# A fused attention and expert kernel: the second stage's input product in seven block products instead of eight

## The chip, the core and the metric

The kernel runs on one core of a Trainium2 chip. The time is the device time of one execution, from the program's start to its end, in microseconds (us). Five engines take part: TensorE (PE, matrix products), VectorE (DVE), ScalarE (ACT), GpSimd (POOL) and SyncE (SP, which here issues DMAs). Each runs its own instructions in order and waits for others through semaphores.

## The reference

Three parts follow each other. Local attention over 4 batches, 8 heads and 768 positions (a window of 96 positions and 8 global ones, with a linear bias) gives x of 3072 tokens by 512. A gated expert then computes `x2 = ((x @ w1) * (x @ w2)) @ w3 @ w_out`, again 3072 by 512. The second expert is where the change lies:

```
def _moe2_ref(x, w_in, w_out):     # w_in 512 x 2048, w_out 2048 x 512
    h = x @ w_in
    g = h * np.cos(h)
    return (g @ w_out).astype(np.float32)
```

All is float32. The kernel keeps that precision by splitting each operand into a high part in the type fp32r and the remainder, and by computing hi·hi + hi·lo + lo·hi: three matmuls for each product (`mm3`, L387 to L394).

## The kernel before, in words

**Stage one** (attention and the first expert) is one loop of 96 slots over 8 blocks of 384 tokens, written out by hand: each slot holds one unit of attention and 24 matmuls of 384 columns, eight slots of a block for `up` (the products with w1 and w2) and four for `down` (with the folded w3 and w_out). The order of every engine is the order in which the code emits; nothing reorders it. Between them `decode` (a generator, L787 to L822) takes a few steps in every slot: it turns the packed weights into float32, for the second stage too, and stores these as `late_w` in DRAM. `up_copy`, `up_mult`, `up_hi` and `up_lo` (L672 to L688) move the results of `up` out of PSUM; `down_out` (L704) splits x2 into its two parts and stores it to DRAM as `x2s`. In the last block, where no attention is left, `late_load` and `late_split` bring back w_in and most of w_out and split them.

**Stage two** (L981 to L1080) takes 6 blocks of 512 tokens. In each, 16 steps: `hidden(J, m)` computes 128 of the 2048 hidden values (12 matmuls of 512 columns: 4 parts of the inner dimension by 3), `gate` computes h·cos(h) from PSUM with three ACT and five DVE operations, and `project`, two steps later, adds the block's contribution to four output banks in PSUM (12 matmuls). `finish` copies the four banks out at the end of each block. All weights stay in SBUF.

PSUM has eight banks of 128 by 512: in stage two four are hidden (`h_ps`) and four output banks (`o_ps`).

## Time and profile before

| | |
|---|---|
| Median of 3 runs | 1170.9 us (1169.41 to 1172.2) |
| Profiled execution, first to last instruction (span) | 1167.0 us |
| Lies around the span (median less span) | 3.9 us |
| PE busy | 1138.3 us (98%) |
| DVE, ACT, POOL busy | 753.8 us (65%), 593.9 us (51%), 112.3 us (10%) |
| Moved by DMA | 131.12 MB |
| Stage two, first to last matmul | 635.48 to 1158.9 us |

The profile has no device time of its own for the profiled execution, only its span; the 3.9 us are the difference to the median. A busy share tells how long an engine had an instruction in it. For PE these overlap (each matmul is recorded with 389 ns, while the next starts after some 226 ns), so the distance between starts tells its rate. The granted clock (PEclk) is the share of full speed that TensorE was allowed: 1.00 is 2.4 GHz and 0.50 is 1.2 GHz.

### The profile page before, as it was taken

The numbers are of one execution on the slowest core, as the hardware profiler recorded it, in microseconds if no ns is written. First come the engines' busy times: TensorE is split into PE (matmuls) and PEld (weight loads), VectorE is DVE, ScalarE is ACT, GpSimd is POOL, SyncE is SP. The second block draws the span as 40 slices with busy tenths as digits, with TensorE's granted clock in tenths as the row PEclk, the third lists the DMA queues.
The fourth block names the chain that finished last, engine by engine and source line by source line (L and its number), as shares of the span: only waits on it lengthen the run. The fifth ranks groups of instructions, "written<-read, shape, count | busy, mean of one in ns | idle before, by whom it ended". The sixth has DMA issues, their size and how long they took to land.

```text
span 1167.0 us, 17288 instructions
## 1 busy us (share of the span) xinstructions
PE 1138.3 (98%) x6178; PEld 985.5 (84%) x6178; DVE 753.8 (65%) x1696; ACT 593.9 (51%) x1309; POOL 112.3 (10%) x197
## 2 busy tenths in 40 slices
PE   5999999999999999999999999999999999999997
PEld 2455899999999999999999888888888888888885
DVE  7797786767676555555344766666666666666664
ACT  6997786666666555555444533333333333333332
POOL 0000001121112111111132300000000000000000
PEclk9899899999999999999999999999999999999999
DMA  8875686575654424343156302002003003000001
GB/s 267 249 227 179 213 298 215 168 222 158 206 169 152 134 88 141 90 151 95 57 173 210 117 1 89 20 1 89 20 1 96 14 1 102 7 1 36 1 1 39
DMA packets 64783, 131.12 MB, mean 112 GB/s; under 512 B 6576, under 2 KB 27312, under 8 KB 64688
## 3 DMA queue, kind: packets, MB, share of 16 engines
q1 hardware_dynamic: 57648, 117.03, 31.2%
q0 software_dynamic: 6528, 12.58, 3.7%
q8 instruction: 51, 0.84, 0.3%
q14 instruction: 44, 0.36, 0.1%
q10 hardware_dynamic: 512, 0.32, 0.1%
HBM read 102.64 MB, written 27.26 MB: 111 GB/s over the span
## 4 chain that ended last, share of the span: by engine, by line
PE 91%; ACT 3%; DMA 2%; DVE 2%; issue 1%; ACTq 0%; SPq 0%; DVEq 0%
PE mm L392 11%; PE mm L394 11%; PE mm L393 11%; PE o_ps L394 7%; PE h_ps L393 7%; PE o_ps L393 7%; PE h_ps L392 7%; PE o_ps L392 7%; PE h_ps L394 7%; PE x_ps L635 3%; PE mm L854 3%; PE pt_ps L608 2%; PE s_ps L553 1%; PE pt_ps L610 1%; PE s_ps L549 1%; DMA raw<-in_winp 1%
## 5 line engine op out<-in xcount | busy, mean ns | idle before, releaser
L1012 ACT ACTIVATE r<-r 128x512 f32<-128x512 f32 x96 | 60.7, 632 | 149.0 <-DVE r L1008 149.0
L1021 ACT CAST g<-r 128x512 fp32r<-128x512 f32 x96 | 59.6, 621 | 139.5 <-DVE r L1017 139.5
L601 POOL TENSOR_SCALAR e<-e,st 128x232 f32<-128x232 f32 x148 | 72.0, 498 | 499.5 <-DVE st L593 479.3
L517 ACT CAST hh<-qk 128x720 fp32r<-128x720 f32 x74 | 58.7, 794 | 118.4 <-PE s_ps L553 113.3
L1014 DVE SCALAR_TENSOR_TENSOR r<-r 128x512 f32<-128x512 f32 x96 | 66.4, 692 | 70.0 <-ACT r L1012 69.9
L1022 DVE TENSOR_TENSOR g<-r,g 128x512 fp32r<-128x512 f32 x96 | 66.5, 692 | 66.0 <-ACT g L1021 66.0
L392 PE MATMUL mm<-xT,wA 128*128 128x384 f32 x256 | 90.6, 354 | 2.3 <-DVE W L863 2.3
L569 DVE CUSTOM_DVE_ANT_0 e<-s_ps,bias 128x232 f32<-128x232 f32 (+1 forms) x192 | 65.5, 378 | 42.3 <-PE s_ps L553 38.9
L580 ACT ACTIVATE e<-e,top 128x232 f32<-128x232 f32 (+1 forms) x192 | 89.3, 468 | 2.3 <-DVE top L569 2.2
L392 PE MATMUL mm<-ab,W 128*128 128x384 f32 x256 | 89.8, 351 | 0.0
L392 PE MATMUL mm<-xT,wB 128*128 128x384 f32 x256 | 89.5, 350 | 0.0
L394 PE MATMUL mm<-xT,wA 128*128 128x384 f32 x256 | 86.9, 340 | 0.0
L393 PE MATMUL mm<-xT,wA 128*128 128x384 f32 x256 | 86.7, 338 | 0.0
L394 PE MATMUL mm<-xT,wB 128*128 128x384 f32 x256 | 86.2, 337 | 0.0
L394 PE MATMUL mm<-ab,W 128*128 128x384 f32 x256 | 86.2, 337 | 0.0
L393 PE MATMUL mm<-ab,W 128*128 128x384 f32 x256 | 85.9, 336 | 0.0
L393 PE MATMUL mm<-xT,wB 128*128 128x384 f32 x256 | 85.8, 335 | 0.0
L1005 DVE SCALAR_TENSOR_TENSOR r<-kt,h_ps 128x512 f32<-128x512 int32 x96 | 65.7, 684 | 28.5 <-ACT kt L1003 28.1
L1003 ACT ACTIVATE kt<-h_ps 128x512 int32<-128x512 f32 x96 | 57.2, 596 | 34.8 <-PE h_ps L394 34.8
L678 DVE TENSOR_TENSOR ab_f<-mm,a_sb 128x384 f32<-128x384 f32 x64 | 35.5, 555 | 55.8 <-PE mm L394 55.8
L1008 DVE SCALAR_TENSOR_TENSOR r<-kt,r 128x512 f32<-128x512 int32 x96 | 66.4, 692 | 3.3
L854 PE MATMUL mm<-wo,w 128*128 128x512 f32 x128 | 63.8, 632 | 4.5 <-DVE wo L348 4.5
(191 smaller groups left out, 3004.3 us busy)
## 6 DMA issues: line engine op xcount, KB each, us to landing
qk<-in_a_qk SPq DMA_DIRECT2D x74, 360.0 KB, 3.1
v<-in_a_v SPq DMA_DIRECT2D x96, 128.0 KB, 2.9
x2s<-x2t SPq DMA_DIRECT2D x32, 384.0 KB, 3.0
raw<-in_w3p SPq DMA_DIRECT2D x16, 512.0 KB, 5.2
raw<-in_winp SPq DMA_DIRECT2D x16, 512.0 KB, 4.3
late_w<-x SPq DMA_DIRECT2D x32, 256.0 KB, 2.1
raw<-in_wo2p SPq DMA_DIRECT2D x16, 512.0 KB, 3.9
raw<-late_w SPq DMA_DIRECT2D x16, 512.0 KB, 4.2
```

The lines of the kernel that those rows point to most:

```text
L392: nc.tensor.matmul(ps, lhsT=l_hi, rhs=r_hi, start=first and i == 0, stop=False)
L393: nc.tensor.matmul(ps, lhsT=l_hi, rhs=r_lo, start=False, stop=False)
L394: nc.tensor.matmul(ps, lhsT=l_lo, rhs=r_hi, start=False, stop=last and i == n - 1)
L569: nc.vector.tensor_tensor_reduce(out=es[n][:, e, :w], in0=sp[:, e, :w], in1=bias[:, 2 * p + e, :], scale=-0.125, scalar=3.0e38, op0=ALU.ad ...
L580: nc.scalar.activation(es[n][:, e, :w], es[n][:, e, :w], ACTF.Exp, bias=top[:, n, e:e + 1], scale=-1.0, accum_out=sts[n][:, 0, e:e + 1],)
L601: nc.gpsimd.tensor_scalar(x, x, st[:, 1, e:e + 1], 1.0, ALU.mult, ALU.mult)
L854: nc.tensor.matmul(W_ps[m], lhsT=wt["w3", c][:, m * 128:(m + 1) * 128], rhs=wt["wo1", k], start=k == 0, stop=k == M1 - 1,)
L1005: nc.vector.scalar_tensor_tensor(out=r, in0=kt, scalar=-C1, in1=ps, op0=ALU.mult, op1=ALU.add)
L1008: nc.vector.scalar_tensor_tensor(out=r, in0=kt, scalar=-C2, in1=r, op0=ALU.mult, op1=ALU.add)
L1012: nc.scalar.activation(r, r, ACTF.Sin, scale=0.5)
L1014: nc.vector.scalar_tensor_tensor(out=r, in0=r, scalar=-2.0, in1=r, op0=ALU.mult, op1=ALU.mult)
L1022: nc.vector.tensor_tensor(out=t[:, 1, :], in0=r, in1=t[:, 0, :].bitcast(F32), op=ALU.subtract)
```

## The change

The product of x2 (512 by 3072) with w_in is written as a 2x2 block product in the Strassen-Winograd form. One **step** takes a pair of hidden blocks (2 x 128), two halves of the inner dimension (2 x 256) and two blocks of 512 tokens (e = 0 and 1). Eight block products would be needed; seven are computed, each of 6 matmuls (`prod`), into four banks a, b, c, d, and the sums are formed by five additions on DVE and two copies on ACT. A round (q) covers 1024 tokens in 8 steps; there are 3 rounds. In a step, `hj` receives the hidden values of the first token block and `gr` those of the second.

- **Weights.** `combos` makes the seven combinations of each pair's four quarters in stage one, splits them and stores them to `a_s` in DRAM. `piece_load` streams them back, 28 pieces of 512 KB in each round. The last weights (`o2`) are split once, stored to `o2s`, and streamed too, 1 MB for each projection task from the ninth on.
- **x2** is stored unsplit. `x2_steps` forms the four differences of the token blocks and splits seven operands, for round 0 in stage one's last block, for rounds 1 and 2 during the round before.
- **Gate.** h now lies in SBUF, and each gate operation covers 128x1024 instead of 128x512. cos comes from Sin, then Square on ACT, with the factor -2 moved to `finish`.
- **Order.** A projection *task* is 24 matmuls, for one token block and one pair. In a step, the gate of the step before is computed and the task of two steps before is projected between the products; the last step of a round (`dense`) has its task behind its products. Then a loop over `b` projects what is left of the round: two tasks of token block 0, then block 1.
- **Stage one's pace.** `decode` takes 3 steps a slot instead of 1.5 from slot 8 on; the buffer `s` of the decoder has one place less; `up_mult` writes in place, into the tile that `up_copy` of the next slot fills again.

```
+PRODS = [
+    ("a", "B11"), ("b", "T2"), ("c", "T1"), ("d", "T3"), ("a", "B21"), ("c", "B22"), ("d", "T4"),
+]
...
-    x2s = dram.tile([MO, 128, 2, NT], F32R, name="x2s")
-    late_w = dram.tile([2, M2, 128, 512], F32, name="late_w")
+    x2s = dram.tile([MO, 128, NT], F32, name="x2s")
+    late_w = dram.tile([M2, 128, 512], F32, name="late_w")
+    a_s = dram.tile([NP * 7 // 2, 128, 2, 2, 2, 128], F32, name="a_s")
+    o2s = dram.tile([M2, 128, 2, 512], F32, name="o2s")
...
+    def combos(i):
+
+        x1, x2 = (xs.pop(("in", 2 * i + e)) for e in range(2))
+
+        def quarter(x, h):
+            return x[:, h * 256:(h + 1) * 256]
+
+        a11, a12, a21, a22 = (quarter(x, h) for x in (x1, x2) for h in range(2))
+        t = attn.tile([128, 256], F32, tag="comb", name="comb", bufs=1)
+        makes = [
+            (0, a11, None), (4, a12, None), (6, a22, None),
+            (3, t, (a11, a21, ALU.subtract)), (2, t, (a21, a22, ALU.add)),
+            (1, t, (t, a11, ALU.subtract)), (5, t, (a12, t, ALU.subtract)),
+        ]
+        for at, x, make in makes:
+            if make:
+                nc.vector.tensor_tensor(out=t, in0=make[0], in1=make[1], op=make[2])
+                yield
+            o = attn.tile([128, 2, 2, 128], F32R, tag="ap", name="ap", bufs=2)
+            v = x.rearrange("p (k c) -> p k c", k=2)
+            nc.scalar.copy(out=o[:, :, 0, :], in_=v)
+            yield
+            nc.vector.tensor_tensor(
+                out=o[:, :, 1, :], in0=v, in1=o[:, :, 0, :].bitcast(F32), op=ALU.subtract
+            )
+            piece, half = divmod(7 * i + at, 2)
+            nc.sync.dma_start(out=a_s[piece, :, half], in_=o.bitcast(F32))
+            yield
+
...
-        ab_f[m] = moe.tile([128, TB], F32, tag="ab_f", name="ab_f", bufs=1)
-        nc.vector.tensor_tensor(out=ab_f[m], in0=mm_ps.pop("b"), in1=a_sb.pop(m), op=ALU.mult)
+        t = ab_f[m] = a_sb.pop(m)
+        nc.vector.tensor_tensor(out=t, in0=mm_ps.pop("b"), in1=t, op=ALU.mult)
...
-        t = x2t[j, m] = moe.tile([128, 2, TB], F32R, tag="x2t", name="x2t", bufs=1)
-        nc.scalar.copy(out=t[:, 0, :], in_=ps)
-        nc.vector.tensor_tensor(
-            out=t[:, 1, :], in0=ps, in1=t[:, 0, :].bitcast(F32), op=ALU.subtract
-        )
+        t = x2t[j, m] = moe.tile([128, TB], F32, tag="x2t", name="x2t", bufs=1)
+        nc.scalar.copy(out=t, in_=ps)
...
-            rings[key] = {"raw": [(misc, 3)], "x": [(attn, 3)], "s": [(attn, 2)]}
+            rings[key] = {"raw": [(misc, 3)], "x": [(attn, 3)], "s": [(attn, 1)]}
...
+                    if k[1] and k[1][0] == "in" and k[1][1] % 2:
+                        yield from combos(k[1][1] // 2)
...
+        def x2_steps(r0, r1):
+
...
+            less(r1, raw("B22"), r0)
+            yield
+            less(r0, r0, raw("B11"))
+            yield
+            yield from x2_split("B11")
+            yield from x2_split("T1", r0)
+            less(r0, raw("B22"), r0)
+            yield
+            yield from x2_split("T2", r0)
+            yield from x2_split("T3", r1)
+            less(r0, raw("B21"), r0)
+            yield
+            yield from x2_split("B21")
+            yield from x2_split("B22")
+            yield from x2_split("T4", r0)
+
...
-                decode(3 if sl < 8 else sl % 2)
+                decode(3 if sl < 8 else 2)
...
+
+        def prod(q, k, i):
+
+            bank, name = PRODS[i]
+            if i < 4:
+                banks[bank] = p_h.tile([128, TB2], F32, tag="h", name="h_ps")
+            n, half = divmod(7 * k + i, 2)
+            w, x = pieces[q, n][:, half], x2c[name]
             mm3(
-                ps,
-                [
-                    (*halves(w, slice(k * 128, (k + 1) * 128)),
-                     x2in[J][:, k, 0, :], x2in[J][:, k, 1, :])
-                    for k in range(MO)
-                ],
-                True, True,
+                banks[bank],
+                [(w[:, e, 0, :], w[:, e, 1, :], x[:, e, 0, :], x[:, e, 1, :]) for e in range(2)],
+                i < 4, True, i >= 4,
             )
 
...
+        class Gate:
+
...
+            def turns(self):
+                self.kt = wts.tile([128, 2, TB2], I32, tag="Wb", name="kt", bufs=4)
+                nc.scalar.activation(self.kt, self.h, ACTF.Identity, scale=INV2PI)
+
+            def rest(self, c):
+                if c == C1:
+                    self.r = wts.tile([128, 2, TB2], F32, tag="Wb", name="r", bufs=4)
+                nc.vector.scalar_tensor_tensor(
+                    out=self.r, in0=self.kt, scalar=-c, in1=self.h if c == C1 else self.r,
+                    op0=ALU.mult, op1=ALU.add,
+                )
+
+            def sine(self):
+                nc.scalar.activation(self.r, self.r, ACTF.Sin, scale=0.5)
+                nc.scalar.activation(self.r, self.r, ACTF.Square)
+
+            def times(self):
+                nc.vector.scalar_tensor_tensor(
+                    out=self.h, in0=self.r, scalar=-0.5, in1=self.h, op0=ALU.add, op1=ALU.mult
+                )
+
+        def g_hi(q, e, k, src):
+            for m in range(2):
+                t = ghl[q, e, 2 * k + m] = wts.tile(
+                    [128, 2, TB2], F32R, tag="Wa", name="g", bufs=4
+                )
+                nc.scalar.copy(out=t[:, 0, :], in_=src[:, m, :])
+
+        def g_lo(q, e, k, src):
+            for m in range(2):
+                t = ghl[q, e, 2 * k + m]
+                nc.vector.tensor_tensor(
+                    out=t[:, 1, :], in0=src[:, m, :], in1=t[:, 0, :].bitcast(F32),
+                    op=ALU.subtract,
+                )
+
+        tasks = [(q, e, k) for q in range(NQ) for e in range(2) for k in range(NP)]
...
+            if t % 2 == 0:
+                osb[0] = wts.tile([128, 2, DM], F32, tag="Wb", name="osb", bufs=4)
...
-                nc.vector.tensor_copy(out=o, in_=o_ps[t])
+                nc.vector.tensor_scalar(o, o_ps[t], -2.0, None, ALU.mult)
...
+        def phase_a(q, k, n, prev):
+
+            late = q == 0
+            if n is not None:
+                o2_load(n + 2)
...
+            dense = k == NP - 1
+            ga, gb = (Gate(gr[prev]), Gate(hj[prev])) if prev else (None, None)
+
...
+            prod(q, k, 0)
+            prod(q, k, 1)
+            gate((ga, "turns"))
+            nc.scalar.copy(out=s1, in_=banks["a"])
+            gate((gb, "turns"), (ga, "rest", C1), (ga, "rest", C2))
+            add(s, banks["b"], s1)
+            gate((ga, "sine"))
+            if n is not None and not dense:
+                project(n, 0)
+            prod(q, k, 2)
+            prod(q, k, 3)
+            if dense:
+                add(v, banks["c"], s)
+                gate((gb, "rest", C1))
+                add(gg[:, 1, :], banks["d"], v)
+                gate((gb, "rest", C2), (gb, "sine"))
+            else:
+                gate((gb, "rest", C1), (gb, "rest", C2), (gb, "sine"))
+                add(v, banks["c"], s)
+                gate((ga, "times"))
+                add(gg[:, 1, :], banks["d"], v)
+                gate((gb, "times"))
+                if prev:
+                    g_hi(*prev[:1], 0, prev[1], hj[prev])
+                    g_lo(*prev[:1], 0, prev[1], hj[prev])
+            if late and 3 <= k < 7:
+                run(late_split(k + 1))
...
+            if n is not None and not dense:
+                project(n, 1)
+            prod(q, k, 4)
+            prod(q, k, 5)
+            prod(q, k, 6)
+            nc.scalar.copy(out=jj[:, 0, :], in_=banks["a"])
+            add(gg[:, 0, :], banks["c"], s)
+            if dense:
+                gate((ga, "times"))
+            add(jj[:, 1, :], banks["d"], s)
+            if dense:
+                gate((gb, "times"))
+                g_hi(*prev[:1], 0, prev[1], hj[prev])
+                g_lo(*prev[:1], 0, prev[1], hj[prev])
+                task(n)
+
...
+            ga, gb = Gate(gr[prev]), Gate(hj[prev])
+            last = q == NQ - 1
+            for b in range(NP + 2 if last else NP):
+                n = 2 * NP * q + NP - 2 + b
+                o2_load(n + 2)
+                if b == 0:
+                    if not last:
+                        x2_loads(q + 1)
+                        r0, r1 = stage_tile(), stage_tile()
+                        nc.sync.dma_start(out=r0, in_=x2_cols("B12", q + 1))
+                        x2_now = x2_steps(r0, r1)
+                    gb.turns()
+                    gb.rest(C1)
+                    gb.rest(C2)
+                    gb.sine()
+                    ga.turns()
+                    ga.rest(C1)
+                    gb.times()
+                    g_hi(q, 0, NP - 1, hj[prev])
+                    ga.rest(C2)
+                    g_lo(q, 0, NP - 1, hj[prev])
+                    ga.sine()
+                    ga.times()
+                if b >= 1 and b - 1 < NP:
+                    g_hi(q, 1, b - 1, gr[q, b - 1])
+                    g_lo(q, 1, b - 1, gr[q, b - 1])
+                if not last and b >= 1:
+                    some(x2_now, 4)
+                    piece_load(q + 1, b - 1)
+                task(n)
```

In the order of PE, a stretch of stage two before: the end of the 12 matmuls of `hidden` and the first of `project`, with one row for each of mm3's three lines.

```order
L392 MATMUL h_ps<-x2in_b,wC 128x512
L393 MATMUL h_ps<-x2in_b,wC 128x512
L394 MATMUL h_ps<-x2in_b,wC 128x512
L392 MATMUL o_ps<-wD,g 128x512
L393 MATMUL o_ps<-wD,g 128x512
L394 MATMUL o_ps<-wD,g 128x512
```

The same engine in the fourth step of round 0 of the change (B and T are the seven operands made of x2, a piece holds combined weights).

```order
L433 MATMUL h_ps<-B_6979,piece 128x512 x6
L433 MATMUL h_ps<-T_7247,piece 128x512 x6
L433 MATMUL o_ps<-wB,g 128x512 x12
L433 MATMUL h_ps<-T_7188,piece 128x512 x6
L433 MATMUL h_ps<-T_7284,piece 128x512 x6
L433 MATMUL o_ps<-wB,g 128x512 x12
L433 MATMUL h_ps<-B_6983,piece 128x512 x6
L433 MATMUL h_ps<-B_6981,piece 128x512 x6
L433 MATMUL h_ps<-T_7445,piece 128x512 x6
```

42 hidden matmuls stand in a step where two token blocks and two hidden blocks took 48, with 24 of projection among them.

In the order of DVE, a gate of one step before, with the last copy of the output banks ahead of it.

```order
L1038 COPY osb<-o_ps 128x512 x2
L1005 SCALAR_TENSOR_TENSOR r<-kt,h_ps 128x512
L1008 SCALAR_TENSOR_TENSOR r<-kt,r 128x512
L1014 SCALAR_TENSOR_TENSOR r<-r 128x512
L1017 SCALAR_TENSOR_TENSOR r<-r,h_ps 128x512
L1022 TENSOR_TENSOR g<-r,g 128x512
```

DVE at the end of round 0's products: from the last addition of the last step to the first two copies of output banks (x2f, B: the operands of the next round).

```order
L1222 TENSOR_TENSOR hj<-h_ps,sv 128x512
L1129 SCALAR_TENSOR_TENSOR hj<-r,hj 128x1024
L1143 TENSOR_TENSOR g<-hj,g 128x512 x2
L1119 SCALAR_TENSOR_TENSOR r<-kt,hj 128x1024
L1119 SCALAR_TENSOR_TENSOR r<-kt,r 128x1024
L1119 SCALAR_TENSOR_TENSOR r<-kt,gr 128x1024
L1129 SCALAR_TENSOR_TENSOR hj<-r,hj 128x1024
L1119 SCALAR_TENSOR_TENSOR r<-kt,r 128x1024
L1143 TENSOR_TENSOR g<-hj,g 128x512 x2
L1129 SCALAR_TENSOR_TENSOR gr<-r,gr 128x1024
L1143 TENSOR_TENSOR g<-gr,g 128x512 x2
L978 TENSOR_TENSOR x2f<-B_8296,x2f 128x1024
```

Behind these come another x2f difference, the subtraction of B (both 128x1024), and then the copies `osb<-o_ps`. Two gates of 1024 columns and the work for the next round stand ahead of the copies, where one gate of 512 columns stood.

In the order of ACT at the same place, from the copy of the last step's bank to the first copies of output banks.

```order
L1266 COPY hj<-h_ps 128x512
L1138 CAST g<-hj 128x512 x2
L1114 ACTIVATE kt<-hj 128x1024
L1125 ACTIVATE r<-r 128x1024
L1126 ACTIVATE r<-r 128x1024
L1114 ACTIVATE kt<-gr 128x1024
L1138 CAST g<-hj 128x512 x2
L1125 ACTIVATE r<-r 128x1024
L1126 ACTIVATE r<-r 128x1024
L1138 CAST g<-gr 128x512 x2
L965 CAST B_8294<-B_8294 128x2x512
L1183 ACTIVATE osb<-o_ps 128x512 x2
```

The turns (kt) of `gr` stand behind Sin and Square of `hj`, and DVE's third wide operation on `gr` ahead of the last one on `hj`.

## Rows read from the trace of the kernel before

**Rows 1.** The page: each engine's busy time.

```profile
PE 1138.3 (98%) x6178; PEld 985.5 (84%) x6178; DVE 753.8 (65%) x1696; ACT 593.9 (51%) x1309; POOL 112.3 (10%) x197
```

**Rows 2.** The page: the chain that ended last, by engine.

```profile
PE 91%; ACT 3%; DMA 2%; DVE 2%; issue 1%; ACTq 0%; SPq 0%; DVEq 0%
```

**Rows 3.** Windows: stretch, busy time of each engine (instructions), granted clock, DMA share, GB/s.

```profile
300.00:366.00 66.00, 66.00 (x462) 64.44 (x461) 45.48 (x138) 42.84 (x108) 12.73 (x24) 1.00 0.56 179
...
600.00:635.00 35.00, 35.00 (x203) 34.75 (x202) 14.72 (x21) 13.86 (x28) 13.39 (x12) 1.00 0.61 199
...
663.00:750.00 87.00, 87.00 (x386) 72.03 (x385) 57.64 (x89) 30.41 (x52) 2.87 (x4) 1.00 0.16 48
```

**Rows 4.** Tile h_ps: durations min/median/max in ns, first and last start, for TensorE.

```profile
L392 PE MATMUL h_ps<-x2in,wA x96: 389/389/389, 663.1 to 1051.9; 128*128 128x512 f32 x96
...
L392 PE MATMUL h_ps<-x2in_b,wA x96: 387/389/501, 750.1 to 1138.9; 128*128 128x512 f32 x96
```

**Rows 5.** Timeline of TensorE: start us, us, engine, line [idle before <-releaser], first projection.

```profile
643.64 0.19 PEld L392 LDWEIGHTS o_ps<-wB,g 128*128 128x128 f32 x1 [0.22 <-ACT g L1021]
...
644.37 0.19 PEld L394 LDWEIGHTS o_ps<-wB,g 128*128 128x128 f32 x1 [0.43 <-DVE g L1022]
```

**Rows 6.** Groups of DVE by shape: xcount | us, mean ns | idle.

```profile
L1008 DVE SCALAR_TENSOR_TENSOR r<-kt,r 128x512 f32<-128x512 int32 x96 | 66.4, 692 | 3.3
...
L1005 DVE SCALAR_TENSOR_TENSOR r<-kt,h_ps 128x512 f32<-128x512 int32 x96 | 65.7, 684 | 28.5 <-ACT kt L1003 28.1
...
L527 DVE TENSOR_TENSOR hh<-qk,hh 64x256 fp32r<-64x256 f32 x74 | 31.3, 423 | 1.0
...
L708 DVE TENSOR_TENSOR x2t<-mm,x2t 128x384 fp32r<-128x384 f32 x32 | 17.8, 555 | 28.9 <-ACT x2t L707 28.9
```

**Rows 7.** Groups of ACT by shape, same columns.

```profile
L1012 ACT ACTIVATE r<-r 128x512 f32<-128x512 f32 x96 | 60.7, 632 | 149.0 <-DVE r L1008 149.0
...
L1021 ACT CAST g<-r 128x512 fp32r<-128x512 f32 x96 | 59.6, 621 | 139.5 <-DVE r L1017 139.5
...
L517 ACT CAST hh<-qk 128x720 fp32r<-128x720 f32 x74 | 58.7, 794 | 118.4 <-PE s_ps L553 113.3 <-ACT s L332 3.3 <-DMA qk<-in_a_qk 1.9
```

**Rows 8.** Timeline of one gate, all engines.

```profile
1144.79 0.39 PE L394 MATMUL h_ps<-x2in_b,wB 128*128 128x512 f32 x1
...
1145.28 0.60 ACT L1003 ACTIVATE kt<-h_ps 128x512 int32<-128x512 f32 x1 [0.57 <-PE h_ps L394]
...
1146.63 0.69 DVE L1008 SCALAR_TENSOR_TENSOR r<-kt,r 128x512 f32<-128x512 int32 x1
...
1147.41 0.63 ACT L1012 ACTIVATE r<-r 128x512 f32<-128x512 f32 x1 [1.54 <-DVE r L1008]
```

**Rows 9.** Windows around two waits of TensorE.

```profile
104.00:107.00 3.00, 0.67 (x4) 0.48 (x4) 2.96 (x7) 3.00 (x8) 0.00 (x0) 1.00 0.31 90
...
119.00:120.00 1.00, 0.72 (x14) 0.47 (x10) 0.43 (x1) 1.00 (x3) 0.00 (x0) 1.00 0.69 279
...
121.00:122.00 1.00, 0.00 (x0) 0.00 (x0) 1.00 (x3) 1.00 (x4) 0.00 (x0) 0.91 0.00 0
...
123.00:128.00 5.00, 5.00 (x20) 4.60 (x17) 3.32 (x10) 3.77 (x9) 0.00 (x0) 0.50 0.51 157
...
128.00:129.00 1.00, 1.00 (x6) 1.00 (x5) 1.00 (x3) 1.00 (x6) 0.00 (x0) 0.68 0.00 0
```

**Rows 10.** Timeline before the end of the second wait.

```profile
121.25 0.46 ACT L674 COPY a_sb<-mm 128x384 f32<-128x384 f32 x1
...
121.64 0.55 DVE L685 TENSOR_TENSOR ab<-ab_f,ab 128x384 fp32r<-128x384 f32 x1
...
122.25 0.48 PE L635 MATMUL x_ps<-pt,v 128*64 128x128 f32 x2 [2.53 <-ACT pt L618]
```

**Rows 11.** Window: the stretch with most DMA.

```profile
150.00:160.00 10.00, 10.00 (x58) 9.08 (x57) 9.21 (x25) 8.98 (x20) 0.00 (x0) 1.00 0.96 323
```

**Rows 12.** The page, DMA issues: out<-in engine op xcount, KB, median us to landing.

```profile
raw<-late_w SPq DMA_DIRECT2D x16, 512.0 KB, 4.2
```

More of the change, by code (lines that the diff above doesn't have):

```diff
@@ L36 @@
 M2 = DF2 // 128
+NQ = NB2 // 2
+NP = M2 // 2
 LEAD = 14
@@ L368, in late_split, with late_store @@
             yield
+    def late_store(pair):
+        for e in range(2):
+            nc.sync.dma_start(out=o2s[2 * pair + e], in_=wt["o2", 2 * pair + e].bitcast(F32))
     def run(steps):
@@ L899, in fused @@
         moe = pool("moe", 2, side="right")
[L902 to L913 removed]
+        x2c, x2_pool = {}, {}
@@ L915, in fused, with piece_load, some @@
+        def piece_load(q, n):
+            if not n < NP * 7 // 2:
+                return
+            t = pieces[q, n] = wts.tile([128, 2, 2, 2, 128], F32R, tag="wA", name="piece")
+            nc.sync.dma_start(out=t.bitcast(F32), in_=a_s[n])
+        w2_steps = None
+        def some(steps, n):
+            for _ in range(n):
+                next(steps, None)
         for j in range(NB1):
@@ L965, in fused @@
                 decode(3 if sl < 8 else 1)
+                if last and 3 <= i < 11:
+                    some(x2_now, 1)
                 if i < M1:
@@ new lines, in fused, with o2_load, finish @@
+        tasks = [(q, e, k) for q in range(NQ) for e in range(2) for k in range(NP)]
+        o2t = {}
+        def o2_load(n):
+            if not NP <= n < len(tasks):
+                return
+            for m in range(2):
+                t = o2t[n, m] = wts.tile([128, 2, 512], F32R, tag="wB", name="o2")
+                nc.sync.dma_start(out=t.bitcast(F32), in_=o2s[2 * tasks[n][2] + m])
+        osb = {}
+        def finish(q, e, t):
+            r0 = (2 * q + e) * TB2 + t * 128
+            if t % 2 == 0:
+                osb[0] = wts.tile([128, 2, DM], F32, tag="Wb", name="osb", bufs=4)
+            o = osb[0][:, t % 2, :]
+            if q == NQ - 1 and e == 1 and t >= 2:
+                if t == 2:
+                    nc.scalar.activation(o, o_ps[t], ACTF.Copy, scale=-2.0)
+                    nc.sync.dma_start(out=out[r0:r0 + 128, :], in_=o)
+                    return
@@ L1080, in fused @@
+        for p in (p_o, p_h, p2, x2cA, wts, edge):
             p.release()
```

249 lines of the change are left out of this document (134 added, 115 removed).

## The prediction, on record before the result

> **What bounds the kernel now.** I read the page's busy times first, then the chain, then stretches. TensorE is busy 98% of the span [rows 1] and makes up 91% of the chain that ended last [rows 2]. In a stretch of stage one it is busy 66.00 of 66 us while DVE has 45.48 and ACT 42.84; in 87 us of stage two it is busy throughout, DVE 57.64, at clock 1.00, which is 2.4 GHz [rows 3]. So matmuls set the time, and the other engines have room: about 30%.
>
> The distance between matmuls comes from a matmul that recurs 16 steps later: 750.1 - 663.1 = 87.0 us for 16 x 24 = 384 matmuls [rows 4], 0.2266 us each. Stage two has 96 x 24 = 2304, half of them hidden (1152).
>
> **What goes.** Seven products instead of eight: 3 rounds x 8 steps x 42 = 1008 hidden matmuls, 144 fewer, of the same shape: 144 x 0.2266 = -32.6 us. The waits in which the first projection stood in before, 0.22 + 0.43 us [rows 5], go with the old start: -0.65.
>
> **What is added beside the matmuls.** DVE's 128x512 operations take 0.69 us, from SBUF or PSUM [rows 6]. No row shows 128x1024. From 64x256 (0.423) to 128x512 (0.692) 256 columns cost 0.269; two more such make 1.23. Ends: 1.08 (no fixed part) and 1.38 (two of 512). On ACT, 512 to 720 columns go from 0.621 to 0.794 [rows 7], so 1024 take 1.05; ends 0.85 and 1.24. I take 1.23 and 1.05, the slopes of the nearest rows; Sin 1.06, Square like the others.
>
> A step then costs DVE five additions, six wide gate operations and two subtractions: 5 x 0.69 + 6 x 1.23 + 2 x 0.69 = 12.2 us, with some 0.5 us of handovers (PE to ACT 0.10, DVE to ACT 0.09 [rows 8]). PE needs 66 x 0.2266 = 15.0 us for a step with a task in it. So steps 2 to 6 of round 0, and 0 to 6 later, are PE's: cost nothing; at 1.38 DVE still has 13.6. ACT has 8.7.
>
> Three places have less PE work than the vector work they stand beside.
>
> *Step 1 of round 0* has no task yet: PE 42 x 0.2266 = 9.5 us against DVE's 12.7. In the step's order, DVE begins at 0.9 (last addition of step 0) and does C1, C2, s, C1, C2, v by 7.2; product 5 was due at 6.8. Then times and addition by 9.1, product 6 late by another 0.5; times by 10.4, two casts on ACT by 11.7, the copy of bank a by 12.3, and the next step's first product, due at 10.6, waits 1.7. Together +2.9.
>
> *End of each round's products.* When the last product ends, PE has two tasks whose operands exist or come in time: 48 x 0.2266 = 10.9 us. The third needs the gate of the step that just ended. Time from the last product's end: rest of a times 0.8, addition 1.5, times 2.75, two casts on ACT 4.05, turns 5.1, C1 and C2 7.65, Sin and Square 9.85, turns of the other gate (ahead in ACT's order) 10.9, C1 of the other gate (ahead in DVE's order) 12.2, times 13.4, cast 14.1. The first two matmuls start at 14.15, the third when C2 of the other gate and the subtraction are through, 15.35. PE idles 3.3 + 0.8 = 4.1 us. With all wide operations at their ends the same sum gives 2.2 and 6.0. Three rounds: +12.3.
>
> *Output banks in rounds 0 and 1.* Behind that, DVE still has a subtraction (16.0), times of `gr` (18.1, after its Sin and Square), two subtractions (19.5), two x2 differences (22.0) and a wide subtraction (23.2). Only then comes the copy of output bank 1 (23.9). PE has finished the task and is at the next token block's bank 1 by 21.0: it waits 2.9 us. Round 2 has no x2 work there. +5.8.
>
> **The clock.** Before, PE did 0.72 us of work in 119 to 120, then stood idle until 122.25 (2.5 us) [rows 9, 10]; the clock fell within 121 to 122 (mean 0.91, so at 121.8), stood at 0.50, 1.2 GHz, and rose within 128 to 129 (mean 0.68, so at 128.6): 6.8 us at half, 3.2 lost with the part in which PE still idled. A wait of like length, 104 to 107 with 0.67 us of work, left it at 1.00 [rows 9]. So I let the 3.3 us wait cost 3.2 more each time. In rounds 0 and 1 the slower PE then finds the output bank nearly free, and 2.9 of the 3.2 is not paid twice: 0.3 + 0.3 + 2.6 = +3.
>
> The Trainium skill, "TensorE: Matmul & The Clock Gate", section "HAM oscillation", says that waits which return in a loop can send the array back to the low clock each time. By that rule every wait above pays, not three: a rival below. The trace shows one wait that did and one that did not.
>
> **Stage one.** `combos` per pair: 11 DVE operations of 256 columns (0.423) and 7 ACT casts (0.621 - 256 x 0.00083 = 0.41); eight pairs: 37 us of DVE, 23 of ACT, over some 64 slots. Gone are 32 subtractions (17.8 us [rows 6]) and w_in's splits. The densest slots decode `o2` three operations a slot instead of 1.5: about 0.9 us more of DVE less 0.2, on 45.48 / 12 = 3.8 a slot: 4.5 of 5.5 us. ACT 3.6 + 0.7. PE hides it. In the last block (35 us, DVE 14.72 and ACT 13.86 [rows 3]) come ten wide operations of x2 (12.3 us on DVE, 6 on ACT) and half the late splits go: about 23 of 35. Hidden too; if a slot's cover were gone, it would cost what a wide operation is, 1.2 us.
>
> One wait grows: `up_copy` now waits until `up_lo` has read the tile it refills. At 121.25 ACT made that copy, while DVE did `up_lo` at 121.64 to 122.19 [rows 10]; the copy of pt behind it, for which PE waited, moves by 0.9. I take +1 for stage one. The fewer `s` buffers make ACT run less far ahead of DVE; cost nothing I can find.
>
> **DMA.** In the projection loop 1.5 MB come per task, 5.44 us: 289 GB/s. 323 GB/s were moved at 0.96 busy in 150 to 160 [rows 11], in smaller transfers; a 512 KB load took 4.2 us to land [rows 12], and these are asked for two tasks (10.9 us) ahead. Hidden.
>
> **Sum against the profiled span.** 1167.0 - 32.6 - 0.65 + 2.9 + 12.3 + 5.8 + 3 + 1 = 1158.8. The runs' median is 3.9 above the span, and the end (last copies and stores) is as before: 1162.7, so 1163 us. No change that could be measured is within 0.2%, 2.3 us: 1168.6 to 1173.2.
>
> **Rivals.**
>
> 1. *The chains at the rounds' ends are short* (wide operations at their low ends, clock stays up): -33.25 + 1 + 1.5 + 3 x 2.2 + 2 x 1.5 = -21, 1150. For it: PE drops out of no stretch of stage two before. Against it: the order of ACT puts both gates in one chain, and 10.9 us of PE work must cover 14. Chance 0.08.
> 2. *The clock takes it back: slower.* Each of the six waits (1.7, 3 x 3.3, 2 x 2.9) halves the clock for 6.8 us and none absorbs another: 6 x 3.2 = 19 instead of 3, 1179. It decides from the fourth stretch that nothing absorbs: (8.2 + 3) / 3.2 = 3.5. For it: 2.5 us sufficed [rows 9]. Against it: the wait that left the clock, and that a slow PE arrives later at the next wait. Chance 0.10.
> 3. *DVE becomes the bound in the steps.* At 1.70 for a wide operation a step is 15.5 us: 20 steps x 0.5, and 3 x 2.8 at the rounds' ends: 1181. Against it: it needs more than two operations of 512 columns cost. Chance 0.06.
> 4. *Stage one pays.* If ACT's casts into the two `ap` buffers wait for stores so that PE loses 0.3 us at each of 56: +17, 1180. For it: two buffers, and stores behind DVE in SP's order. Against it: 64 slots for 56 stores, PE fully covered now. Chance 0.09.
>
> That the change doesn't remove the matmuls is excluded: PE's order has 42 a step.
>
> **How the numbers follow.** The forecast has 0.67, by itself 1155 to 1170 (the rounds' ends between their bounds 3 x 1.9 either way, one stretch of low clock more or less). The range takes in rival 1's time and the smaller outcomes of 2 to 4: 1150 to 1176. Faster: 0.08 of rival 1 and 0.62 of the forecast, 0.70. Within 0.2%: 0.05 of the forecast and 0.05 of rivals 2 to 4 where they come out small, 0.10. Slower: the other 0.20 of these.
>
> **What would show it.** Right: 1008 hidden matmuls at 0.2266 us; in the steps no wait of PE; three waits of 3 to 5 us at the rounds' ends, ended by ACT's cast and DVE's subtraction `g`, two of up to 3 us ended by DVE's `osb`, one of 1.7 us ended by ACT's copy of bank a; a half clock after the long ones; stage two about 512 us long instead of 523. Wrong: wide operations away from 1.23 and 1.05, PE waiting for `piece` or `o2` loads, slots of stage one longer than 5.5 us, or half clock after each wait.

## The result, and the profile after

The changed kernel takes 1160.26 us (median of 4 runs, 1159.74 to 1161.33) against 1171.55 us (1169.41 to 1173.93): ratio 0.9912, 95% interval 0.9893 to 0.993. By the ratio that is some 10 us faster, by the medians 11.3; the forecast was 1163 us, with a range of 1150 to 1176. The profiled execution has a span of 1158.0 us (before 1167.0) and took 1159.94 us.

The page after, its busy times and the chain that ended last [rows 1, 2]:

```profile
PE 1113.6 (96%) x6034; PEld 962.1 (83%) x6034; DVE 781.8 (68%) x1657; ACT 681.2 (59%) x1370; POOL 81.8 (7%) x165
...
PE 85%; DVE 7%; ACT 5%; issue 1%; DMA 1%; ACTq 0%; DVEq 0%; SPq 0%
```

TensorE is still the bound, but the chain now has 12% of DVE and ACT in it where it had 5%. The table takes the span apart by the starts of the matmuls in the two traces; the matmuls of stage one are the same 3872 in the same order, so the k-th, counted from 0, can be set against the k-th.

| Stretch | before, us | after, us | difference |
|---|---|---|---|
| start to the 400th matmul (before 123, after 128 us) | 123.30 | 128.13 | +4.8 |
| 400th to 3700th | 482.17 | 480.34 | -1.8 |
| 3700th to the first of stage two (last block) | 30.01 | 35.86 | +5.9 |
| stage two, first to last matmul start | 523.05 | 506.02 | -17.0 |
| rest of the span | 8.46 | 7.64 | -0.8 |

So the gain in stage two is 17 us and stage one gives back 8.9. (In the second stretch a wait of 0.7 us of before, at 160 to 170, is gone, and less of the half clock behind 122 lies in it.) What TensorE waited for longest, without the start of the program (columns: waiting, releaser, us in total, times, longest):

```profile
PE o_ps L433 <- ACT g L1138: 6.9, 3, 2.3
...
PE mm L433 <- DVE W L901: 4.0, 1, 4.0
PE pt_ps L650 <- ACT e L641: 4.0, 2, 3.0
PE x_ps L677 <- ACT pt L660: 3.6, 1, 3.6
PE mm L433 <- ACT ab L724: 2.1, 1, 2.1
PE o_ps L433 <- DVE osb L1178: 1.7, 1, 1.7
PE mm L433 <- DVE a_sb L720: 1.4, 1, 1.4
PE o_ps L433 <- DVE g L1143: 0.9, 3, 0.3
```

The first row and the last are the rounds' ends (three of 2.3 us, three of 0.3), `osb` is an output bank, and the other five rows lie in stage one. Before the change `ab` and `a_sb` did not appear among the waits, and `W` was 2.3 us, `e` 2.7 and `pt` 3.3 in two waits, the longer one 2.53 [rows 10].

Windows after, as in [rows 9] (stretch, busy us of PE, PEld, DVE, ACT, POOL with instructions, granted clock, DMA share, GB/s):

```profile
105.00:110.00 5.00, 2.09 (x7) 2.10 (x8) 4.04 (x8) 3.69 (x7) 0.00 (x0) 0.76 0.37 108
110.00:115.00 5.00, 5.00 (x27) 4.55 (x26) 3.95 (x11) 1.75 (x3) 0.00 (x0) 0.89 0.43 142
625.00:630.00 5.00, 2.74 (x15) 2.16 (x14) 3.50 (x6) 2.98 (x5) 1.27 (x1) 0.99 0.18 72
630.00:635.00 5.00, 5.00 (x21) 5.00 (x22) 4.75 (x4) 2.46 (x4) 1.30 (x1) 0.67 0.59 230
760.00:765.00 5.00, 2.73 (x7) 1.91 (x8) 3.99 (x6) 3.67 (x6) 0.00 (x0) 0.80 0.01 2
765.00:770.00 5.00, 5.00 (x21) 4.06 (x20) 4.86 (x6) 2.87 (x6) 0.00 (x0) 0.86 0.00 0
930.00:935.00 5.00, 3.86 (x16) 2.91 (x17) 3.98 (x6) 4.80 (x7) 0.00 (x0) 1.00 0.01 3
...
1100.00:1105.00 5.00, 4.70 (x14) 3.69 (x15) 3.27 (x5) 2.83 (x4) 0.00 (x0) 0.66 0.00 0
```

A granted clock of 0.76 and 0.89 in two windows of 5 us is 0.24 x 5 / 0.5 + 0.11 x 5 / 0.5 = 3.5 us at 0.50, 1.2 GHz, behind the `W` wait. The same sum gives 3.4 us behind the `ab` wait of the last block (0.99, 0.67), 3.4 behind the end of round 0 (0.80, 0.86), none behind that of round 1 (1.00) and 3.4 behind that of round 2 (0.66).

### The profile page after: what moved, and what is told of

Its sections match the earlier page's. It is cut to its first block, busy times and chain, and to the rows that moved or that the text cites. A ratio compares the mean times of both kernels' runs of the same rounds, so it can differ in the third digit from the quotient of the medians.

```text
span 1158.0 us, 17393 instructions
## 1 busy us (share of the span) xinstructions
PE 1113.6 (96%) x6034; PEld 962.1 (83%) x6034; DVE 781.8 (68%) x1657; ACT 681.2 (59%) x1370; POOL 81.8 (7%) x165
## 4 chain that ended last, share of the span: by engine, by line
PE 85%; DVE 7%; ACT 5%; issue 1%; DMA 1%; ACTq 0%; DVEq 0%; SPq 0%
PE mm L433 34%; PE h_ps L433 19%; PE o_ps L433 19%; PE x_ps L677 4%; PE mm L892 3%; PE pt_ps L650 2%; PE s_ps L595 1%; PE pt_ps L652 1%; PE s_ps L591 1%; DVE r L1119 1%; PE s_ps L583 1%; DMA nraw<-in_n_global 1%; DVE hj L1129 1%; ACT kt L1114 1%; DVE x2f L978 1%
## 5 line engine op out<-in xcount | busy, mean ns | idle before, releaser
L433 PE MATMUL o_ps<-o,g 128*128 128x512 f32 x960 | 226.2, 392 | 7.1 <-ACT g L1138 4.6
L433 PEld LDWEIGHTS o_ps<-o,g 128*128 128x128 f32 x960 | 180.8, 189 | 47.3 <-ACT g L1138 5.4
L433 PE MATMUL mm<-xT,wA 128*128 128x384 f32 x768 | 149.9, 345 | 4.0 <-DVE W L901 4.0
L433 PE MATMUL mm<-ab,W 128*128 128x384 f32 x768 | 149.0, 344 | 2.3 <-ACT ab L724 2.1
L433 PE MATMUL mm<-xT,wB 128*128 128x384 f32 x768 | 147.4, 341 | 1.4 <-DVE a_sb L720 1.4
L433 PE MATMUL h_ps<-T,piece 128*128 128x512 f32 x576 | 141.7, 389 | 0.1
L433 PEld LDWEIGHTS mm<-xT,wA 128*128 128x128 f32 x768 | 134.6, 192 | 6.3 <-DVE W L901 4.4
L433 PEld LDWEIGHTS mm<-ab,W 128*128 128x128 f32 x768 | 133.2, 190 | 5.2 <-ACT ab L724 2.4
L433 PEld LDWEIGHTS mm<-xT,wB 128*128 128x128 f32 x768 | 131.7, 188 | 3.8 <-issue 2.1
L433 PEld LDWEIGHTS h_ps<-T,piece 128*128 128x128 f32 x576 | 108.0, 188 | 23.2 <-DVE gr L1222 0.5
L433 PEld LDWEIGHTS h_ps<-B,piece 128*128 128x128 f32 x432 | 80.9, 188 | 17.1 <-DVE vv L1222 0.4
L720 DVE TENSOR_TENSOR a_sb<-mm,a_sb 128x384 f32<-128x384 f32 x64 | 35.5, 555 | 45.1 <-PE mm L433 43.8
```

The source lines that it names most:

```text
L433: nc.tensor.matmul(ps, lhsT=l, rhs=r, start=first and i + e == 0, stop=last and i == n - 1 and e == 2, skip_group_check=more,)
L720: nc.vector.tensor_tensor(out=t, in0=mm_ps.pop("b"), in1=t, op=ALU.mult)
```

## The experiments

Each starts from the changed kernel, whose median is 1160.3 us; most are one edit, e5 and e8 to e10 are several. All have four runs; the ratio is to the kernel before, run on the same chip. The medians of the kernel before lie between 1169.3 and 1171.6 us in the sets of runs, and the intervals of e1, e3, e4, e6 and e7 hold the changed kernel's ratio, 0.9912. So the times alone do not tell these five from the changed kernel; there the stretches and waits of the traces decide. "Interval" is the distance of two matmul starts.

**e1: a place for `s` in the early pool.**

```
-            rings[key]["x"].append((early, 4))
-            rings[key]["s"].append((early, 2))
+            rings[key]["x"].append((early, 3))
+            rings[key]["s"].append((early, 3))
```

> One edit: the decoder's buffer s gets back its fourth place (and x gives up one of seven for it). The changed kernel's median is 1160.3 us. Theory: the wait of the first up products (4.0 us at 104 to 108, before the change 2.3) comes from ACT, whose s conversion waited for DVE's sum with the three places and stood ahead of the W casts. Then the wait falls to about 2.3 us, the 3.4 us of half clock behind it and the 1.0 us wait at 118.5 go: 3 to 4 us less, 1156.5. Rival: the denser decoding itself (three steps a slot) delays the W casts, whatever the ring: no change, 1160, with ACT then waiting on x instead.

Measured 1159.57 us, 0.9916 (0.9891 to 0.9941). The interval before the first up product is 4.37 us (4.39 after the change): nothing moved, and by the expectation's own words this spoke for the rival. But the trace of the changed kernel shows ACT in the wait (timeline rows: start us, us, engine, line, [idle before <-releaser]):

```profile
105.99 0.66 ACT L340 ACTIVATE s<-raw 128x512 int32<-128x512 uint32 x1 [1.58 <-DVE x L356]
106.56 2.03 ACT L900 CAST W<-mm 128x512 fp32r<-128x512 f32 x4
...
107.91 3.78 PE L433 MATMUL mm<-xT,wA 128*128 128x384 f32 x12 [4.03 <-DVE W L901]
```

ACT's conversion into `s` stands 1.58 us waiting for the sum (L356) that frees the previous `s`, and the `W` casts stand behind it. The rings of words beyond the first 30 have only the place in the long-lived pool, and there the change had gone from two to one. The experiment had enlarged the other ring.

**e5: two places for `s` where it counts** (and one less in the early pool; x2t shares a_sb's one place).

```
-            rings[key] = {... "s": [(attn, 1)]}
+            rings[key] = {... "s": [(attn, 2)]}
-                rings[key]["s"].append((early, 2))
+                rings[key]["s"].append((early, 1))
```

> The experiment with s asked the wrong buffer: the words from the 31st on use only the place in the long-lived pool, and that is the one that went from two to one. One edit: two places there, one in the early pool (x2t moves into a_sb's place to pay for it; a_sb keeps one). Theory: ACT's s conversion no longer waits 1.6 us for DVE's sum ahead of the W casts; the interval between matmuls at 104 (4.4 us in the changed kernel, about 2.6 before the change) falls to about 2.6, the half clock behind it and the 1.0 us wait at 118 may go: 2 to 4 us less in the first 130 us. Rival: the denser decoding puts more of ACT's and DVE's work ahead of the W casts, whatever the buffers: the interval stays at 4.4. The shared x2t may cost a few tenths at each of seven block borders, told apart by its place.

Measured 1156.56 us, 0.9874 (0.9852 to 0.9895). The same place:

```profile
103.75 0.66 ACT L340 ACTIVATE s<-raw 128x512 int32<-128x512 uint32 x1
...
106.32 2.00 PE L433 MATMUL mm<-xT,wA 128*128 128x384 f32 x10 [2.33 <-DVE W L901]
```

No wait of ACT ahead of the casts, TensorE waits 2.33 us as before the change, no half clock follows, and the 400th matmul starts at 124.20 us instead of 128.13; at the end of stage one 3.1 of these 3.9 us are left. The theory holds, the rival falls: the decoding is as dense as before.

**e6: the last chunk's decode steps behind the W casts.**

```
+            if c < 2 * M1 - 1:
                 decode(1)          # twice, ahead of wmm
 ...
+            if c == 2 * M1 - 1:
+                decode(2)          # behind wmm(0..3)
```

> One edit: in the last of the 16 chunks that make W, the two decode steps that stood ahead of the W casts stand behind them (ACT: one x and one s conversion; DVE: one sum and one shift). Both theories for the wait (the one s place; the denser decoding) expect the interval of 4.4 us at 104 to fall, to 2 or below, since both put the same s conversion in ACT's way; the half clock behind it then goes too. 3 to 4 us less in the first 130 us. If the interval stays at 4 or more, the W casts and subtractions themselves (2.0 and 2.5 us for four) are the wait.

Measured 1157.83 us, 0.9901 (0.988 to 0.9923). The waits:

```profile
PE pt_ps L650 <- ACT e L641: 7.4, 2, 4.4
...
PE mm L433 <- DVE W L901: 2.0, 1, 2.0
```

The `W` wait is 2.0 us, but one of 4.4 us for the softmax (`e`) stands at 118 us in its place, again behind an `s` conversion that waited 2.22 us. At the 400th matmul 0.9 us of gain is left, where 3 to 4 were expected; of the rest of the 2.4 us, 1.6 lie in stage two, which the edit does not touch (the clock, see e8). An order mends one spot; the one buffer holds up a later word instead.

**e2: two places for a_sb** (shared with x2t, same memory).

```
-        a_sb[m] = moe.tile([128, TB], F32, tag="a_sb", name="a_sb", bufs=1)
+        a_sb[m] = moe.tile([128, TB], F32, tag="a_sb", name="a_sb", bufs=2)
-        t = x2t[j, m] = moe.tile([128, TB], F32, tag="x2t", name="x2t", bufs=1)
+        t = x2t[j, m] = moe.tile([128, TB], F32, tag="a_sb", name="x2t", bufs=2)
```

> One edit: a_sb has two places (shared with x2t, so the memory is the same). Theory: in stage one's last block the one place ties ACT and DVE into a loop (up_mult, up_hi, up_lo, up_copy, then the x2 and o2 casts) that is longer than PE's 5.2 us slot in slots with a late_split; then the wait of 1.4 us at 621 goes, the one of 2.1 us at 629 shrinks by about 0.5, and the half clock behind may stay: 1.5 to 3.5 us less, about 1158. Rival: DVE is held up by GpSimd's half of late_split (its row 1.77 us instead of 0.69): then the wait at 621 stays, within 0.3 us, and the time is 1160.

Measured 1153.76 us, 0.9864 (0.9839 to 0.9888). To see what it acts on, the last block of the changed kernel:

```profile
615.54 0.56 DVE L727 TENSOR_TENSOR ab<-a_sb,ab 128x384 fp32r<-128x384 f32 x1 [0.58 <-ACT ab L724]
616.19 0.48 ACT L716 COPY a_sb<-mm 128x384 f32<-128x384 f32 x1 [0.68 <-DVE ab L727]
616.56 1.05 ACT L965 CAST T<-x2f 128x1024 fp32r<-128x1024 f32 x1
...
617.64 1.23 DVE L967 TENSOR_TENSOR T<-x2f,T 128x1024 fp32r<-128x1024 f32 x1 [1.55 <-ACT T L965]
618.73 1.29 POOL L424 TENSOR_TENSOR wB<-raw,wB 128x512 fp32r<-128x512 f32 x1 [7.38 <-ACT wB L420]
618.79 1.77 DVE L424 TENSOR_TENSOR wB<-raw,wB 128x512 fp32r<-128x512 f32 x1
620.49 0.54 DVE L720 TENSOR_TENSOR a_sb<-mm,a_sb 128x384 f32<-128x384 f32 x1
...
621.09 2.37 PE L433 MATMUL mm<-xT,wB 128*128 128x384 f32 x12 [1.36 <-DVE a_sb L720]
...
628.07 0.55 DVE L720 TENSOR_TENSOR a_sb<-mm,a_sb 128x384 f32<-128x384 f32 x1
...
629.21 1.25 PE L433 MATMUL mm<-ab,W 128*128 128x384 f32 x2 [2.11 <-ACT ab L724]
```

`up_copy` (L716) cannot start before `up_lo` (L727) has read the tile it refills; the cast of T on ACT stands behind it, the subtraction of T on DVE waits for the cast, the split of o2 for that, and behind all of these DVE comes to `up_mult` (L720), for which TensorE waits. One turn of this loop is 6.1 us: 4.95 from L727 at 615.54 to L720 at 620.49, and 1.1 from there through the cast to L727 again. A slot of TensorE in this block is 24 x 0.1734 = 4.2 us (the expectation had 5.2, a slot with attention in it). With two places no row for `a_sb` is left, and of the second wait, 2.1 us, the second line here. The first is the wait for `pt` at 127 us, 3.6 us in the changed kernel:

```profile
PE x_ps L677 <- ACT pt L660: 2.5, 1, 2.5
...
PE mm L433 <- ACT ab L724: 0.7, 1, 0.7
```

The last block takes 31.23 us instead of 35.86, with no half clock in it: 4.6 us, where 1.5 to 3.5 were expected. 1.6 more of the 6.5 us are in stage two, where in this execution the clock fell at the ends of rounds 0 and 1 instead of 0 and 2, so that it lay over the wait for the bank. The edit changes nothing there, and e1 and e6 have the same 1.6 us; they are no gain of the edit.

**e3: no GpSimd in late_split.**

```
-            w_lo(key, nc.gpsimd if e else nc.vector)
+            w_lo(key, nc.vector)
```

> One edit: both halves of late_split on DVE, none on GpSimd. Rival of the experiment before (contention with GpSimd): the wait of 1.4 us at 621 falls under 0.4 and the time by about 1 us or more, 1159. Theory (the loop through the one a_sb): DVE saves 0.4 us where it was held up (2 x 0.69 for 1.77) and loses 0.69 where it was not, ahead of the wait at 629: one wait 0.4 smaller, the other 0.7 larger, 1160 to 1161.

Measured 1161.28 us, 0.9921 (0.9896 to 0.9947). The two waits of the last block, 2.1 and 1.4 in the changed kernel:

```profile
PE mm L433 <- ACT ab L724: 2.7, 1, 2.7
...
PE mm L433 <- DVE a_sb L720: 1.1, 1, 1.1
```

One 0.3 smaller, the other 0.6 larger, as the loop through a_sb has it. The contention itself is real: DVE's split at 618.79 took 1.77 us while GpSimd's at 618.73 ran 1.3 us. The Trainium skill, "SBUF — State Buffer", section "Who interferes with whom", says that a VectorE instruction with two inputs in SBUF contends with a GpSimd one that reads SBUF, by an exclusive lock. The trace agrees in the main: 1.23 us until GpSimd's end and 0.54 after it, where a split without such company takes 0.69 (spans on GpSimd are rough). It is a cost on DVE's row, and not what TensorE lost here.

**e4: the order of the two gates at a round's end.**

```
                     gb.turns()
+                    ga.turns()
                     gb.rest(C1)
                     gb.rest(C2)
                     gb.sine()
-                    ga.turns()
                     ga.rest(C1)
                     gb.times()
                     g_hi(q, 0, NP - 1, hj[prev])
-                    ga.rest(C2)
                     g_lo(q, 0, NP - 1, hj[prev])
+                    ga.rest(C2)
                     ga.sine()
```

> One edit, the order of the two gates at each round's end: the turns of gr stand ahead of Sin and Square of hj on ACT, and on DVE the two subtractions g of hj ahead of C2 of gr. Theory: the waits of 2.3 + 0.3 us at 762, 931 and 1099 come from that order; they fall to about 0.3 + 0.25 each, and with them the two stretches of half clock (1.7 us each). But DVE reaches the copies of the output banks no earlier, so in rounds 0 and 1 PE waits there for what it gained: about 4 us at 770 (before 0.3) and 4 us at 940 (before 1.9). Net about 4 us less, nearly all in round 2: 1156.5. Rival: the vector work as a whole is what ends late, so that the order changes nothing: 1160. Second rival: the copies are not the next limit, then 10 us less, 1150.

Measured 1159.0 us, 0.9904 (0.9879 to 0.9929). The end of round 1 in the changed kernel, at 935.77 the first of three wide operations ahead of DVE's copies:

```profile
925.67 1.06 ACT L1126 ACTIVATE r<-r 128x1024 f32<-128x1024 f32 x1
926.64 1.04 ACT L1114 ACTIVATE kt<-gr 128x1024 int32<-128x1024 f32 x1
927.71 1.22 DVE L1119 SCALAR_TENSOR_TENSOR r<-kt,gr 128x1024 f32<-128x1024 int32 x1 [3.17 <-ACT kt L1114]
928.86 1.22 DVE L1129 SCALAR_TENSOR_TENSOR hj<-r,hj 128x1024 f32<-128x1024 f32 x1
...
930.16 1.14 ACT L1138 CAST g<-hj 128x512 fp32r<-128x512 f32 x2 [2.48 <-DVE hj L1129]
...
930.84 0.73 PE L433 MATMUL o_ps<-o,g 128*128 128x512 f32 x2 [2.30 <-ACT g L1138]
...
935.77 1.22 DVE L978 TENSOR_TENSOR x2f<-B,x2f 128x1024 f32<-128x1024 f32 x1
...
939.50 1.28 DVE L1178 TENSOR_SCALAR osb<-o_ps 128x512 f32<-128x512 f32 x2
...
940.24 0.96 PE L433 MATMUL o_ps<-o,g 128*128 128x512 f32 x3 [1.74 <-DVE osb L1178]
```

ACT does the turns of `gr` only after the Square of `hj`, DVE stands 3.17 us for them, and `times` of `hj` (928.86), for which nothing is missing since 926.7, comes behind. With the other order the waits for `g` are 0.6 us together instead of 7.8, and the banks take them over in rounds 0 and 1:

```profile
PE o_ps L433 <- DVE osb L1178: 5.3, 2, 2.7
...
PE o_ps L433 <- ACT osb L1183: 2.4, 3, 1.1
...
PE o_ps L433 <- ACT g L1138: 0.6, 3, 0.2
```

The intervals there are 1.5 and 3.1 us in both rounds. That is the expectation; the time is 2.5 us above it, some 1.6 of them since the clock fell behind the 3.1 us of round 1. By the time alone the first rival, 1160, could not be told apart; it falls by the waits, which moved, and by round 2, which has no x2 work and loses 3.4 us less (1.6 of them a half clock). The second falls in rounds 0 and 1.

**e7: the x2 steps behind the task that finishes the bank.**

```
-                if not last and b >= 1:
+                if not last and b > 1:
                     some(x2_now, 4)
                     piece_load(q + 1, b - 1)
                 task(n)
+                if not last and b == 1:
+                    some(x2_now, 4)
+                    piece_load(q + 1, b - 1)
```

> One edit: at each round's end the first four x2 steps of the next round stand behind the task that finishes the first token block, instead of ahead of it. Theory: the wait for an output bank (round 1: interval 2.13, round 0 hidden by the half clock) is due to three wide operations (3.7 us) ahead of DVE's copy; it goes in both rounds, and the 2.7 us intervals stay: 2 us less in round 1, up to 0.3 in round 0, 1158. Rival: the copy waits for the gate of gr, not for the x2 work: unchanged, 1160.

Measured 1158.5 us, 0.9903 (0.9885 to 0.9921). No row for `osb` is left among the waits, so the theory holds on whose wait it is. Stage two takes 504.03 us instead of 506.02, the 2 us expected, but not where they were expected: 0.4, 0.9 and 0.6 us at the three rounds' ends. In round 1 the wait of 2.0 us is gone and a half clock has come; in round 2 the edit changes nothing.

**e8: e4 and e7 together.**

> Two edits together: the gates' order at the round's end (which by itself moved the wait to the output banks, intervals of 1.5 and 3.1 us) and the x2 steps behind that task. Theory: what the first edit moved was x2 work ahead of the copies; without it the intervals at the banks fall to under 1 us, no half clock is left in stage two, and stage two takes 506.0 - 3 x 2.5 - 3.3 - 2 + 1 = 494 us: 1149. Rival: the gate of gr alone still holds DVE until the copies are late: 1.5 to 2 us stay at each of two banks, stage two 498, 1153.

Measured 1150.82 us, 0.9837 (0.9819 to 0.9856). All that TensorE waits for at the banks and for `g` in stage two:

```profile
PE o_ps L433 <- ACT g L1138: 0.6, 3, 0.2
PE o_ps L433 <- ACT osb L1183: 0.5, 3, 0.2
```

The clock stays at 1.00 until the last matmuls, and stage two takes 495.81 us (expected 494). By themselves the two edits gave 1.8 and 2.0 us, together 10.2. Where they do so is told by the time lost at each round's end (matmul intervals less 0.2266 us, bank waits and half clock included; a star marks an end with a half clock):

| | round 0 | round 1 | round 2 |
|---|---|---|---|
| changed kernel | 5.2 * | 5.2 | 4.8 * |
| e2 (no edit here) | 5.2 * | 5.2 * | 3.2 |
| e4 | 5.2 | 6.8 * | 1.4 |
| e7 | 4.8 * | 4.3 * | 4.2 * |
| e8 | 1.8 | 1.8 | 1.4 |

In rounds 0 and 1 each wait stands behind the other: e4 alone loses 1.5 us there (a half clock behind the longer wait for the bank), e7 alone gains 1.4, both together 6.8. Round 2 has no x2 work, and e4's edit gains its 3.4 us there alone (1.8 if no half clock had been there before).

**e9 and e10: the mended versions.** Both have e8's edits and this one; e9 adds e5's, e10 e2's.

```
-                if last and 3 <= i < 11:
+                if last and 3 <= i < 11 and i != 7:
                     some(x2_now, 1)
                     ...
 ...
                     up_lo(j, i - 1)
+                if last and i == 8:
+                    some(x2_now, 1)
+                    run(late_split(2))
```

> Four edits together: two places for s (as in e5), the last x2 step and late_split of slot 7 of the last block moved behind up_lo of the next slot, and both edits of the rounds' ends (as in e8). Theory: the 2.1 us wait at 629 comes from what stands on DVE and ACT ahead of the last up_mult, so it falls under 0.5 and the half clock behind it goes, while the wait of 1.4 us at 621 stays (it needs the second place of a_sb): last block 35.9 to 32.6 us. With first 130 us 3 to 4 shorter and stage two 495.8: 1160.3 - 3.2 - 3.2 - 10.2 = 1143.7. Rival for the last block: ACT and DVE simply have too much there, so that the moved work delays the next slots by as much: 35.9 stays, 1147.

> As the experiment before, but with two places for a_sb instead of two for s (there is memory for one of them). Theory: both waits of the last block go (alone the second place gave 31.2 us; with the tail of slot 7 moved another 0.8): 30.4 us, the first 130 us stay as in the changed kernel, stage two 495.8: 1160.3 - 5.4 - 10.2 = 1144.7. Rival: as above, the last block keeps 31.2 or more.

Measured: e9 1143.97 us, 0.977 (0.9745 to 0.9794), last block 32.64 us; e10 1144.31 us, 0.9781 (0.9765 to 0.9797), last block 30.37 us, with no wait in it. In e9 the two waits of the last block are as expected: 1.3 us for `a_sb` kept, 0.5 for `ab` left of 2.1. Its `W` wait is 2.3 us as in e5, but here the clock halves behind it (granted clock 0.86 in 105 to 110 us and 0.79 in 110 to 115, 1.00 in both in e5), so the shorter wait does not always keep the clock up. In e10 the first 130 us, expected unchanged, are 1.5 us shorter, with the wait for `pt` at 2.5 us again.

Both beat the changed kernel by 16 us, and the sums of the expectations (1143.7 and 1144.7) are met within 0.4 us.

## Why the prediction was right, and where it only seemed so

The number came out by luck, by two errors of 8 us that cancel: stage two was forecast 9.25 us shorter and is 17.0, stage one 1 us longer and is 8.9. (The "about 512 us" among the signs does not follow from the forecast's terms, which give 523.05 - 9.25 = 513.8.) Term by term, stage two from the matmul starts (each interval less 0.2266 us):

| Term | forecast | measured |
|---|---|---|
| 144 matmuls gone | -32.6 | -32.6 |
| old start's waits | -0.65 | -0.4 |
| step 1 of round 0 | +2.9 | +0.9 |
| rounds' ends | +12.3 | +9.5 (3 x 3.15) |
| output banks | +5.8 | +2.4 (0.4, 2.0) |
| clock in stage two | +3 | +3.1 |
| stage one | +1 | +8.9 |
| rest of the span | 0 | -0.8 |
| median less span | 3.9 | 1.9 (profiled run) |

The first row is 2304 less 2160 matmuls, both at 0.2266 us; the rows of stage two add up to 17.1 us of the 17.0. The last row is an error of 2 us of its own: in every run whose span is on record the time lies 1.7 to 2.0 us above it, so the 3.9 set a median against a profiled execution that was some 2 us faster than it.

**Right.** The duration of an operation of 1024 columns, estimated from narrower shapes [rows 6, 7]:

```profile
L1119 DVE SCALAR_TENSOR_TENSOR r<-kt,r 128x1024 f32<-128x1024 int32 x48 | 58.8, 1225 | 1.4
...
L1125 ACT ACTIVATE r<-r 128x1024 f32<-128x1024 f32 x48 | 51.0, 1062 | 34.9 <-DVE r L1119 34.9
```

1.225 us where 1.23 was taken, and 1.062 for Sin where 1.06 was. So the steps are TensorE's in all three rounds, as forecast (behind the first two products of step 2 no more than 0.1 us of waits up to a round's end), and in stage two no load was waited for. The chain at the rounds' ends is the one that was written down, link by link: turns of `gr` behind Sin and Square, C1 of `gr` ahead of `times`; e4 shows that this order is the cause. That a slow clock would swallow the wait for the bank is what happened: round 0 fell to half clock and waited 0.4 us there, round 1 did not and waited 2.0, both lost 5.2 us in all, and e7 shows whose wait it is. The price of `up_copy` waiting for `up_lo` at 121 us, +0.9, was right too: TensorE's wait for `pt` there is 3.60 us instead of 2.53, and 2.5 again with two places, where the copy no longer stands behind `up_lo` (e2, e10).

**Mis-sized.** The rounds' ends were 3.15 us, not 4.1. In round 1 the two tasks at hand begin here:

```profile
917.49 11.04 PE L433 MATMUL o_ps<-o,g 128*128 128x512 f32 x48
```

The chain from there to the first matmul behind the wait (930.84) took 13.35 us, not 14.15. No link stands out: most are 0.05 to 0.13 us shorter, for an operation often starts up to 0.1 us before the record of the one ahead of it ends (the Square at 925.67 lasts 1.06 us, the turns behind it start at 926.64), where the forecast set them end to end. The rest is the third matmul's wait, 0.5 us instead of 0.8. The stretch of half clock was taken as 6.8 us long, from the one case in the trace of before, and is 3.4 behind the rounds' ends; it fell twice instead of three times.

**Failed: step 1 of round 0.** "the next step's first product, due at 10.6, waits 1.7" did not occur:

```profile
664.05 1.54 PE L433 MATMUL h_ps<-B,piece 128*128 128x512 f32 x6
...
664.90 0.58 ACT L1266 COPY hj<-h_ps 128x512 f32<-128x512 f32 x1
```

The first product of step 2 starts at 664.05, before ACT copies bank a at 664.90. It cannot use that bank, nor c and d, which DVE reads later still (665.71 and 666.31): it gets bank b, which DVE's addition had read by 657.8. The four banks go round by when they come free. Only the second product waits for the copy, 0.1 us. A list of which bank each product gets would have shown it.

**Failed: stage one.** "The fewer `s` buffers make ACT run less far ahead of DVE; cost nothing I can find." They cost 3.9 us before the 400th matmul and 3.1 by the end of stage one (e5): not through ACT's work, of which there is room, but through what stands behind a waiting conversion in ACT's order. And "Hidden too", for the last block with 23 of 35 us on DVE, counted busy time where a loop through one buffer decides: `up_copy` waiting for `up_lo` was seen, but priced at its one place at 121 us and not where wide casts stand behind it (e2: 4.6 us). The last block became 5.9 us longer, where the forecast's price for a slot without cover was 1.2. In the 35 us there was room; in the slots with a split there was none.

**The rivals.** Short chains: no, 9.5 us. The clock after every wait: no. It fell at 16 of the 21 rounds' ends of the seven executions that keep the 2.7 us interval, and at none of the twelve where an interval of 0.6 us is left. The Trainium skill, "TensorE: Matmul & The Clock Gate", section "HAM oscillation", says that waits that return can do it each time; its example is of longer waits, for transfers. The trace agrees that returning waits can, not that each does. Where it fell and a wait for the bank followed, that wait took it in, as forecast against this rival. DVE as the bound: no, wide operations are 1.22. Stage one pays: yes, by half of what that rival said, but not through the stores of `ap`, whose casts had no idle time before them (here the 32 from `comb`):

```profile
L382 ACT CAST ap<-comb 128x256 fp32r<-128x256 f32 x32 | 12.8, 401 | 0.0
```
